# The opening of a Fourier-mixing and MLP kernel: x ahead of the weights, weights converted inside the first chunk, plain products there

## The chip, the cores and the metric

One core of one Trainium2 chip. The metric is the time of one execution on the device in microseconds (us). Spans in the traces run from the first to the last instruction and are 1.7 to 1.8 us shorter than the times. In the profile's rows PE is TensorE (PEld its weight loads), DVE is Vector, ACT is ScalarE, POOL is GpSimd and SP is SyncE; a name with q, such as ACTq, is that engine issuing transfers.

## The reference

x is (8, 3008, 256). A Fourier transform over the sequence and over the features, real part kept, gives 24,064 rows of 256. These pass an MLP with 2048 hidden units:

```python
X = np.fft.fft(np.fft.fft(x, axis=1), axis=2).real.astype(np.float32)
h = X.reshape(B * S, D) @ w_in          # weights are float64
g = h * np.clip(h + 3.0, 0.0, 6.0) / 6.0
return (g @ w_out).astype(np.float32)
```

## The kernel before

Four pairs of sequences are done in turn. For a pair: x and its mirrored rows ("partners") are read and folded; stage 1 of the sequence transform gives z, which goes to DRAM (`zd`) and comes back regrouped as g; stage 2 gives q. The transform over features is folded into the first weights (W1, and a column WN). Then come 12 chunks of 8 steps. A step is the first layer (`mlp1`: four matmuls of 256 columns, then Vector and ACT for the activation) and the second layer (`mlp2`): a 2 x 2 block product by seven products instead of eight, with additions on GpSimd (`combine`) and mixed weight blocks.

The weights arrive as float64, in 16 pieces. ACT reads out the exponent bits (`exponent_a`), PE and ACT make them a float32 power of two (`exponent_b`, `exponent_c`), Vector assembles the mantissa and multiplies (`mantissa`, `join`). Before, almost all of this ran in the opening, with x interleaved; only the end of piece 15 and the last mixing fell into the first chunk:

```python
for c in range(NXC):                       # eight chunks of x
    if c + 2 < NXC: load_x(first, c + 2)
    load_w(c + 2)                          # a weight piece beside each chunk
    fold_first(first, c) ...               # Vector
    on_scalar(c); on_vector(c)             # exponent, mantissa of piece c
    for i in range(XC // 2): stage1_first(first, c, i)
    on_tensor(c)
load_g(first, 0)
for j in range(NXC, 15):                   # the other pieces
    ...                                    # (cut)
for i in range(2): stage2(first, 0, i)
...                                        # the chunks, 8 steps each
def exponent_b(j):
    ex = ps_h.tile([P, WB], F32, tag="uv", name="ex")
    for i in range(2):
        nc.tensor.matmul(ex[:], E[:, i], PM[:, j % 2, i].bitcast(F16), ...)
```

Of the kernel before, what the change touches and what calls it, by code (L numbers as in the profile page):

```python
# [51 lines left out]

PROD = ("P1", "P2", "-P4", "P5", "P7", "-P6", "P3")
# [3 lines left out]
def kernel(  # L57
# [51 lines left out]
    F = consts.tile([PR + 2, 5 * PZ + NP * NXC + 1], F32, name="F")  # L109
# [17 lines left out]
    def x_tile(pr, i):  # L127
        pool, tag = xpool, "x"
        if pr.p == 0 and 4 <= i < 13:
            pool, tag = ((apool, "a"), (cpool, "c"), (spool, "t"))[(i >= 8) + (i >= 11)]  # L130
        return pool.tile([PR + 2, XC, D], F32, tag=tag, name="xt")
# [8 lines left out]
    def load_forward(pr, c):  # L140
        xt = x_tile(pr, 2 * c)

        nr = PR + 2 if pr.p < NP - 1 else PR
        rows = x_pn[pr.p * PR:pr.p * PR + nr]
        n = XC if c < NXC - 1 else XC - 1
        nc.gpsimd.dma_start(out=xt[0:nr, 0:n, :], in_=rows[:, c * XC + 1:c * XC + 1 + n, :])
        if n < XC:
            nc.gpsimd.dma_start(out=xt[0:nr, n:XC, :], in_=rows[:, 0:1, :])
        pr.x[c] = xt

    def load_partners(pr, c):
        xr = x_tile(pr, 2 * c + 1)
# [31 lines left out]
    def fold_first(pr, c):  # L184
        xt, xr = pr.x[c][0:PR], pr.xr[c][0:PR]
        r = xr[:, ::-1, :]
        y = ypool.tile([PR, XC + 1, D], F32, tag="y", name="y")
        tt = nc.vector.tensor_tensor
        tt(y[:, 0:XC, 1:P], xt[:, :, D - 1:P:-1], r[:, :, 1:P], op=AL.add)
        tt(xt[:, :, 1:P], xt[:, :, 1:P], r[:, :, D - 1:P:-1], op=AL.add)  # L190
        tt(xt[:, :, 0:P + 1:P], xt[:, :, 0:P + 1:P], r[:, :, 0:P + 1:P], op=AL.add)
        pr.y[c] = y

    def stage1_first(pr, c, i):
        sl = slice(2 * i, 2 * i + 2)
        a, b = pr.x[c][0:PR, sl, :], pr.y[c][:, sl, 1:P]
        ps = bank([P, 2, D], "ps1")
        for k, (f, m, c0) in enumerate([(F[0:PR, 0:PZ], a[:, :, 0:P + 1], 0), (F[0:PR, 0:PZ], b, 1),
                                        (F[0:PR, 0:PZ], a[:, :, 1:P], P + 1), (FN[0:PR], b, P + 1)]):
            nc.tensor.matmul(ps[0:PZ, :, c0:c0 + m.shape[2]], f, m, start=(k == 0), stop=(k > 0),  # L200
                             skip_group_check=True)
        evict_z(pr, c, i, ps)
        if i == XC // 2 - 1:
            del pr.x[c], pr.xr[c]
# [9 lines left out]
    def stage1(pr, c, i):  # L214

        y = pr.y[c]
        ps = bank([P, 2, D], "ps1")
# [10 lines left out]
        evict_z(pr, c, i, ps)  # L228

    def evict_z(pr, c, i, ps):  # L230
        if i == 0:

            pool, tag = (gpool, "g") if pr.p == 0 and c % 3 == 2 else (zpool, "z")
            pr.z[c] = pool.tile([PZ, XC, D], F32, tag=tag, name="z")
            if c == 0:
                pr.zd = dpool.tile([2, NK1, 2, NS, D], F32, tag="zd", name="zd")
                pr.zq = dpool.tile([2, NK1, 2, NS], F32, tag="zq", name="zq")
        z = pr.z[c]
        nc.scalar.copy(z[:, 2 * i:2 * i + 2, :], ps[0:PZ])  # L239
        if i == XC // 2 - 1:  # L240
            nc.sync.dma_start(
                out=pr.zd[:].rearrange("b k c n d -> (b k c) n d")[:, c * XC:(c + 1) * XC, :],
                in_=z[:],
            )
            turn_column(pr, c, z)
            del pr.y[c], pr.z[c]
# [4 lines left out]
    def turn_column(pr, c, z):  # L251
        n = XC if c < NXC - 1 else XC - 1
        zc = zpool.tile([PZ, XC], F32, tag="zc", bufs=4, name="zc")
        nc.scalar.activation(zc[:, 0:n], z[:, 0:n, P], AF.Identity, scale=F[0:PZ, 5 * PZ + NP * NXC:])
        cs = slice(c * XC, c * XC + n)
        nc.sync.dma_start(out=pr.zq[:, :, ::-1, cs].rearrange("b k c n -> (b k) c n"), in_=zc[:, 0:n])
        if n < XC:
            nc.sync.dma_start(out=pr.zq[:, :, :, c * XC + n].rearrange("b k c -> (b k c)"), in_=z[:, n, P])


    def load_g(pr, gr):
        g = gpool.tile([P, 2 * KK, D + 1], F32, tag="g", name="g")
        ks = slice(gr * 2 * KK, (gr + 1) * 2 * KK)
        gb = [g[b * N2:(b + 1) * N2] for b in range(2)]
        for b in range(2):
            nc.sync.dma_start(out=gb[b][:, :, 0:D], in_=pr.zd[b].rearrange("k c n d -> (c n) k d")[:, ks, :])
        for b in range(2):
            nc.sync.dma_start(out=gb[b][:, :, D], in_=pr.zq[b].rearrange("k c n -> (c n) k")[:, ks])
# [36 lines left out]
    class Chunk:  # L305
# [3 lines left out]
        def __init__(self, pr, ck):  # L309
            self.pr, self.ck = pr, ck  # L310
            self.last = ck == NCK - 1
            self.final = self.last and pr.p == NP - 1
# [81 lines left out]

    def mlp2(ch, fc):
# [78 lines left out]
    FN = wpool.tile([PR + 2, PZ], F32, tag="FN", name="FN")  # L474
# [8 lines left out]
    raw, exs, fracs, w = {}, {}, {}, {}  # L483

    def load_w(j):
        kind, n, i = PIECES[j]
        st = wpool.tile([P, 2 * WB], I32, tag="st", bufs=4, name="st")
# [17 lines left out]
    def exponent_a(j):  # L505
        top = raw[j][:].bitcast(I16).rearrange("p (n four) -> p n four", four=4)[:, :, 3]
        for i in range(2):
            low = PM[:, j % 2, i].bitcast(U8).rearrange("p (n two) -> p n two", two=2)[:, :, 0]
            nc.scalar.activation(low, top, AF.Identity, bias=bias[:, i:i + 1], scale=(1 - 2 * i) / 16.0)  # L509

    def exponent_b(j):
        ex = ps_h.tile([P, WB], F32, tag="uv", name="ex")
        for i in range(2):
            nc.tensor.matmul(ex[:], E[:, i], PM[:, j % 2, i].bitcast(F16), start=(i == 0), stop=(i == 1))  # L514
        exs[j] = ex
# [4 lines left out]
    def mantissa(j):  # L520
# [3 lines left out]
        top = wpool.tile([P, WB], I32, tag="top", bufs=2, name="top")  # L524
# [5 lines left out]
    def join(j):  # L530
# [8 lines left out]
        b12 = wpool.tile([P, 2, P], F32, tag="b12", bufs=2, name="b12")[:] if i == 0 else None  # L539
        for h, g in enumerate((block(n, 0), b12) if i == 0 else (block(n, 1), block(n, 6))):  # L540
            f, e = (t.rearrange("p (c q h e) -> h p c q e", c=2, h=2, e=DH)[h] for t in (frac, ex))
            nc.vector.tensor_tensor(g.rearrange("p c (q e) -> p c q e", e=DH), f, e, op=AL.mult)
        if i == 0:
            w[PIECES[j]] = b12
# [4 lines left out]
    def use_pair(j):  # L549
        kind, n, _ = PIECES[2 * j]  # L550
        if kind == "in":
            fold_w_in(n)
        else:
            mix_w_out(n)

    def mix_w_out(j):

        b12 = w.pop(("out", j, 0))
        g = [block(j, i) for i in range(7)]
        tt = nc.vector.tensor_tensor  # L560
        tt(g[3], g[0], b12, op=AL.subtract)
        tt(g[5], g[6], g[3], op=AL.add)
        tt(g[2], g[5], g[1], op=AL.subtract)
        tt(g[4], g[6], b12, op=AL.subtract)

    def fold_w_in(n):

        cs = slice(n * WB, (n + 1) * WB)
        ws = [w.pop(("in", n, i)) for i in range(2)]
        sums = []  # L570
        for blk in range(2):
            ps = bank([P, WB], "wps")
            for i in range(2):
                nc.tensor.matmul(ps[:], C[:, i, blk * P:(blk + 1) * P], ws[i], start=(i == 0), stop=(i == 1))  # L574
            sums.append(ps)

        def copy():
            for blk in range(2):
                nc.scalar.copy(W1[:, blk, cs], sums[blk][:])
            nc.sync.dma_start(out=wn[n:n + 1], in_=W1[P - 1:P, 1, cs])  # L580

        copies.append(copy)


    def load_wn(n):
        nb = WB // P
        nc.sync.dma_start(out=WN[:, n * nb:(n + 1) * nb], in_=wn[n].rearrange("(j p) -> p j", p=P))
# [6 lines left out]
    def keep_awake(n):  # L594
        ps = ps_h.tile([P, 2 * TB], F32, tag="uv", name="awake")
        for i in range(n):
            nc.tensor.matmul(ps[:], ones[:], Z[:], start=True, stop=True)  # L597
# [4 lines left out]
    keep_awake(6)  # L602
    nc.sync.dma_start(out=F[:], in_=c_stage1)
# [4 lines left out]
    PM = wpool.tile([P, 2, 2, WB], I16, tag="PM", name="PM")  # L608
    nc.vector.memset(PM[:].rearrange("p j i n -> p (j i n)").bitcast(I32), 0x64006400)
    nc.vector.tensor_copy(IX[:], F[:, 5 * PZ:5 * PZ + NP * NXC])  # L610
    nc.scalar.mul(FN[:], F[:, 0:PZ], -1.0)
# [3 lines left out]
    nc.sync.dma_start(out=C[:], in_=dim[:, :, 0:D])  # L615
    E = wpool.tile([P, 2, P], F16, tag="E", name="E")
    nc.scalar.copy(E[:], CE[:])
    for b in range(2):
# [3 lines left out]
    wn = dpool.tile([NWI, WB], F32, tag="wn", bufs=1, name="wn")  # L622


    load_forward(first, 0)
    load_partners(first, 0)
    load_w(0)
    load_x(first, 1)
    load_w(1)
# [3 lines left out]
    pending, copies = [], []  # L633

    def on_scalar(j):
        for i in pending:
            exponent_c(i)
        if j is not None:
            exponent_a(j)
        while copies:  # L640
            copies.pop(0)()

    def on_vector(j):
        if j is not None:
            mantissa(j)
        for i in pending:
            join(i)

    def on_tensor(j):
        if j is not None:  # L650
            exponent_b(j)
        done = pending.pop() if pending else 0
        if done % 2:
            use_pair(done // 2)
        if j is not None:
            pending.append(j)

    for c in range(NXC):
        if c + 2 < NXC:
            load_x(first, c + 2)  # L660
        load_w(c + 2)
        if c < NXC - 1:
            fold_first(first, c)
        else:
            for part in range(2):
# [185 lines left out]
```

## Time and profile before

| Kernel before | |
|---|---|
| time, median of 4 runs (first chip) | 1980.1 us |
| last operation of x's last fold starts | 49.4 us |
| first step: second half of its fused addition with WN | 82.4 us |
| E: eight steps of the first chunk done, with the first layer of two more | 132.2 us |
| from E to the end of the span (1978.3) | 1846.1 us |

Vector's timeline has the first step (columns: start, length, engine, line, operation, output <- inputs, shapes, count):

```profile
82.03 0.86 DVE L339 SCALAR_TENSOR_TENSOR s<-qn,WN,u 128x256 f32<-128x256 f32 x2
```

The two instructions of 0.47 us are merged into one row, so the second starts near 82.4. PE's timeline has E, where the last row below starts:

```profile
129.18 1.46 PE L403 MATMUL acc<-a,G 128*128 128x256 f32 x6
130.48 1.89 PE L403 MATMUL acc<-c,G 128*128 128x256 f32 x8
132.21 1.02 PE L227 MATMUL ps<-y,F 94*96 94x512 f32 x2
```

### The profile page before, as it was taken

The numbers are of one execution on the slowest core, as the hardware profiler recorded it, in microseconds if no ns is written. First come the engines' busy times: TensorE is split into PE (matmuls) and PEld (weight loads), VectorE is DVE, ScalarE is ACT, GpSimd is POOL, SyncE is SP. The second block draws the span as 40 slices with busy tenths as digits, with TensorE's granted clock in tenths as the row PEclk, the third lists the DMA queues.
The fourth block names the chain that finished last, engine by engine and source line by source line (L and its number), as shares of the span: only waits on it lengthen the run. The fifth ranks groups of instructions, "written<-read, shape, count | busy, mean of one in ns | idle before, by whom it ended". The sixth has DMA issues, their size and how long they took to land.

```text
span 1978.3 us, 27746 instructions
## 1 busy us (share of the span) xinstructions
PE 1949.1 (99%) x9178; PEld 1685.4 (85%) x9178; DVE 1433.5 (72%) x2775; ACT 687.9 (35%) x1164; POOL 1414.2 (71%) x1604
## 2 busy tenths in 40 slices
PE   8899999999999999999999999999999999999998
PEld 5588888888998888888898888888889888888887
DVE  5677767776787776776777776777678777777776
ACT  6533333333333333333333333333333333333332
POOL 4277778786687787777768877778667667666765
PEclk9999999999999999999999999999999999999999
DMA  9502211111111111221111221212110101111000
GB/s 307 136 26 61 51 41 46 49 49 35 27 36 51 41 49 48 54 59 24 36 32 30 63 55 44 56 41 54 37 22 23 30 14 25 26 24 28 17 20 20
DMA packets 149701, 93.31 MB, mean 47 GB/s; under 512 B 121739, under 2 KB 135055, under 8 KB 149558
## 3 DMA queue, kind: packets, MB, share of 16 engines
q1 hardware_dynamic: 139294, 57.86, 12.2%
q0 software_dynamic: 9472, 33.49, 5.9%
q8 instruction: 72, 1.18, 0.2%
q14 instruction: 71, 0.58, 0.1%
q10 hardware_dynamic: 792, 0.20, 0.0%
HBM read 54.19 MB, written 37.33 MB: 46 GB/s over the span
## 4 chain that ended last, share of the span: by engine, by line
PE 93%; DVE 2%; ACT 1%; issue 0%; DMA 0%; SPq 0%; DVEq 0%; ACTq 0%
PE acc L403 56%; PE v L334 16%; PE u L334 16%; PE ps L284 2%; PE ps L227 2%; DVE a L379 1%; DVE s L339 1%; ACT t L376 0%; ACT PM L509 0%; DVE o L461 0%; PE wps L574 0%; DVE u L360 0%; PE ps L224 0%; PE ex L514 0%; PE awake L597 0%
## 5 line engine op out<-in xcount | busy, mean ns | idle before, releaser
L393 POOL TENSOR_TENSOR c<-a 128x512 f32<-128x512 f32 (+1 forms) x383 | 478.2, 1248 | 431.4 <-PE acc L403 369.3
L403 PE MATMUL acc<-c,G 128*128 128x256 f32 (+1 forms) x3072 | 712.0, 375 | 0.0
L376 ACT ACTIVATE t<-u,half 128x512 f32<-128x512 f32 (+1 forms) x384 | 261.0, 680 | 1100.5 <-DVE u L349 1018.7
L403 PEld LDWEIGHTS acc<-c,G 128*128 128x128 f32 x3072 | 577.5, 190 | 72.7
L339 DVE SCALAR_TENSOR_TENSOR s<-qn,WN,u 128x256 f32<-128x256 f32 (+1 forms) x768 | 330.0, 471 | 354.3 <-PE u L334 354.0
L403 PE MATMUL acc<-a,G 128*128 128x256 f32 (+1 forms) x2304 | 551.2, 375 | 0.0
L403 PEld LDWEIGHTS acc<-a,G 128*128 128x128 f32 x2304 | 433.8, 190 | 55.9
L334 PE MATMUL v<-q,W 127*128 127x256 f32 (+1 forms) x1536 | 390.1, 376 | 4.4 <-DVE a L379 4.4
L334 PE MATMUL u<-q,W 128*128 128x256 f32 (+1 forms) x1536 | 388.3, 375 | 2.4 <-DVE a L379 2.1
L379 DVE SCALAR_TENSOR_TENSOR a<-t,u 128x512 f32<-128x512 f32 (+2 forms) x448 | 263.7, 600 | 104.9 <-ACT t L376 102.1
L334 PEld LDWEIGHTS u<-q,W 128*128 128x128 f32 x1536 | 285.7, 190 | 58.2 <-issue 14.8
L334 PEld LDWEIGHTS v<-q,W 127*128 127x128 f32 x1536 | 288.7, 190 | 45.1 <-DVE a L379 4.1
L393 POOL TENSOR_TENSOR c<-c,a 128x256 f32<-128x256 f32 (+1 forms) x383 | 274.8, 717 | 30.0
L393 POOL TENSOR_TENSOR c<-a,c 128x256 f32<-128x256 f32 (+1 forms) x383 | 274.6, 717 | 30.1
L349 DVE TENSOR_TENSOR u<-s,v 128x512 f32<-128x512 f32 x352 | 245.0, 696 | 37.7 <-PE v L334 0.8
L379 DVE SCALAR_TENSOR_TENSOR a<-t,v 128x512 f32<-128x512 f32 (+1 forms) x480 | 263.2, 564 | 0.0
L376 ACT ACTIVATE t<-v,half 128x512 f32<-128x512 f32 (+1 forms) x384 | 260.5, 678 | 0.0
L351 DVE TENSOR_TENSOR v<-v,s 128x512 f32<-128x512 f32 x352 | 243.7, 692 | 0.0
L393 POOL TENSOR_TENSOR r<-w,e 128x256 f32<-128x256 f32 (+1 forms) x94 | 90.8, 987 | 3.7
L411 ACT ACTIVATE e<-acc 128x512 f32<-128x512 f32 (+2 forms) x190 | 86.3, 545 | 3.4 <-PE acc L403 3.3
L461 DVE STREAM_TRANSPOSE o<-r 128x256 f32<-128x256 f32 (+1 forms) x192 | 72.5, 414 | 0.2
L239 ACT COPY z<-ps 96x512 f32<-96x512 f32 x64 | 37.2, 582 | 83.7 <-PE ps L227 65.2
(91 smaller groups left out, 780.2 us busy)
## 6 DMA issues: line engine op xcount, KB each, us to landing
out_dram<-o SPq DMA_DIRECT2D x746, 32.0 KB
zd<-z SPq DMA_DIRECT2D x32, 384.0 KB
g<-zd SPq DMA_DIRECT2D x48, 256.0 KB
xt<-in_x_dram POOLq DMA_DIRECT2D x21, 384.0 KB, 4.1
qn<-qd SPq DMA_DIRECT2D x19, 256.0 KB
st<-in_moe_w_in_dram POOLq DMA_DIRECT2D x8, 512.0 KB, 9.1
st<-in_moe_w_out_dram POOLq DMA_DIRECT2D x8, 512.0 KB, 5.1
xt<-in_x_dram POOLq DMA_DIRECT2D x7, 376.0 KB, 3.9
```

The source lines that it names most:

```text
L227: nc.tensor.matmul(ps[0:PZ], F[0:PR, 0:PZ], y[:, 2 * i:2 * i + 2, :], start=True, stop=True)
L284: nc.tensor.matmul(ps[:, blk, u * P:n].rearrange("p (b k) -> p b k", b=2), g[:, kk, blk * (P + 1):blk * (P + 1) + P], T[:, :, gr, blk, kk, ...
L334: nc.tensor.matmul(ps[:, i, 0:nq], W1[r, blk, f * P:(f + 1) * P], q[r, blk, of:of + nq], start=True, stop=True)
L339: nc.vector.scalar_tensor_tensor(s[:, i, 0:nq], qn[:, of:of + nq], WN[:, f:f + 1], u[:, i, 0:nq], op0=AL.mult, op1=AL.add)
L349: nc.vector.tensor_tensor(u[:], s[:], v[:], op=AL.add)
L351: nc.vector.tensor_tensor(v[:], v[:], s[:], op=AL.subtract)
L376: nc.scalar.activation(t, h, AF.Relu, bias=half[:], scale=scale)
L379: nc.vector.scalar_tensor_tensor(dst, t, 1.0, h, op0=AL.min, op1=AL.mult)
L393: (eng or nc.gpsimd).tensor_tensor(out, in0, in1, op=AL.add)
L403: nc.tensor.matmul(ch.acc[i // 2][:, i % 2, 0:ch.n], G[:, i, fc, :], mv, start=(fc == 0 and i % 2 == 0), stop=(fc == NF - 1), skip_group_c ...
L411: nc.scalar.mul(ch.e[:, k:i + 1, 0:ch.n], ch.acc[i // 2][:, 0:i + 1 - k, 0:ch.n], 1.0 / WS)
L461: nc.vector.transpose(o[:, 0:n // DH, h], ch.r[:, m, h, 0:n].rearrange("p (j i) -> p j i", i=DH))
```

## The change

The intent is to reach the first step earlier. x is read ahead of all weights; only the first four pieces are converted before the first step, and the other twelve inside the first chunk. Weights 4 and later are read only when the first group's g is back. Of z only the rows of the first group are written at once; the rest waits (`later`). Exponents of odd pieces from the fifth on are made by a subtraction on Vector instead of two matmuls. In the first chunk the second layer is done by eight plain products (four matmuls of 512 columns), since the mixed weight blocks aren't ready; mixing moves from Vector to GpSimd. WN is filled straight from W1's last row by small transfers, not over DRAM.

```diff
+    for c in ORDER[0:3]: load_x(first, c)
+    for k, c in enumerate(ORDER):
+        for part in range(2): fold(first, c, part, nc.vector)
+        for i in range(XC // 2): stage1(first, c, i)
+        keep_awake(1)
+        if k + 3 < NXC: load_x(first, ORDER[k + 3])
+        ...                                   # weights 0 to 3 behind the last x
     load_g(first, 0)
+    nc.gpsimd.tensor_copy(seen[:], first.g[0][:, 0, 0:1])   # GpSimd waits for g
+    for j in range(4, 8): load_w(j)
+    ...                                       # pieces 0 to 3 converted
     for i in range(2): stage2(first, 0, i)
+    for dst, src in later[2:6] + later[0:2] + later[6:]:
+        nc.scalar.dma_start(out=dst, in_=src)               # deferred z
     spread(first, 0)
+    fold_w_in(*folds.pop(1)); copy_all()      # W1's second half, its WN column
     def exponent_b(j):
+        if j >= 4 and j % 2:
+            nc.vector.tensor_tensor(exs[j][:], pm[0], pm[1], op=AL.subtract)
+            return
+    def mlp2_first(ch, fc):
+        for h in range(2):
+            for f in range(2):
+                nc.tensor.matmul(ch.acc[h][:], G[:, (B11, B12, B21, B22)[2 * f + h], fc, :], a[:, :, f], ...)
     # in the copy() of fold_w_in:
+            nc.sync.dma_start(out=WN[:, f:f + 1], in_=W1[P - 1:P, 1, f * P:(f + 1) * P])
     # further down:
+    DUE = [(6, 7), (8, 9, 10), (11, 12), (13, 14), (15,), (), (), ()]   # pieces per step
+            t = 2 * late + (9 - late // 4) * c   # next pair's x, in the first pair later and closer
     # (many lines cut)
```

## The prediction

> **What bounds the kernel now.** I read the page first: busy shares, then the 40 slices, then the chain that ended last.
>
> ```profile
> PE 1949.1 (99%) x9178; PEld 1685.4 (85%) x9178; DVE 1433.5 (72%) x2775; ACT 687.9 (35%) x1164; POOL 1414.2 (71%) x1604
> ...
> PE   8899999999999999999999999999999999999998
> ...
> PE 93%; DVE 2%; ACT 1%; issue 0%; DMA 0%; SPq 0%; DVEq 0%; ACTq 0%
> ```
>
> PE is 93% of the chain and the first slices alone are thin. Next, busy time by stretches of the span (columns: stretch, length, busy time and count of PE, PEld, DVE, ACT, POOL, then clock, DMA share, GB/s):
>
> ```profile
> 0.00:46.00 46.00, 42.98 (x154) 25.59 (x154) 23.93 (x53) 31.25 (x49) 19.80 (x32) 1.00 0.99 301
> 46.00:92.00 46.00, 35.59 (x115) 19.46 (x114) 30.28 (x65) 25.80 (x43) 9.12 (x12) 0.90 0.62 168
> 92.00:132.00 40.00, 38.54 (x185) 33.71 (x184) 30.98 (x52) 12.28 (x21) 25.77 (x28) 0.99 0.05 16
> 132.00:1978.00 1846.00, 1831.94 (x8730) 1606.62 (x8728) 1348.34 (x2607) 618.59 (x1054) 1359.51 (x1533) 1.00 0.16 39
> ```
>
> After 132 us (the end of the first chunk: its eighth group of second-layer matmuls runs 129.18 to 132.21) PE lacks only 14 of 1846 us. The change leaves that part's work as it is, so the time after is 1846 plus the moment E at which the first chunk is done. The question is how far E moves from 132.2.
>
> Three landmarks before E, from the timeline by engine: the last fold of x starts at 46.56 and ends at 49.5; Vector's first step of the first chunk starts at 82.0; E = 132.2. In the first 46 us DMA is full (share 0.99). In the second stretch it is ACT, PE and Vector in turn, seen in the chain in order of time:
>
> ```profile
> 68.81 0.47 issue
> 69.28 1.41 ACT PM L509 x2
> 70.69 0.04 issue
> 70.73 0.39 PE ex L514
> ...
> 71.64 1.41 ACT PM L509 x2
> 73.05 0.04 issue
> 73.09 0.39 PE ex L514
> ...
> 74.00 1.41 ACT PM L509 x2
> 75.41 0.04 issue
> ```
>
> ACT's two exponent instructions come every 2.36 us: that is the price of one of the 16 weight pieces while nothing useful can run on PE.
>
> **What the Trainium skill says.** "DMA: Bandwidth & Descriptors", Issuing engines are not separate DMA queues: transfers of all engines interleave on the same 16 DMA engines, whoever issued them. The trace agrees: an indirect read of x takes a median of 5.1 us to land over the whole span and 12.5 us in the first 90 us, beside the weights. So moving weights behind x buys x time. "TensorE: Matmul & The Clock Gate", Part 1: after about 3.4 us of idleness the array runs at half clock until busy again for about as long. The trace agrees: after 3.3 us idle the two-pass 512-column matmul at 49.17 took 1.99 us, against 1.02 us at 132.21. "SBUF — State Buffer", Who interferes with whom: a Vector operation with two SBUF inputs contends with GpSimd reading SBUF. Agrees: Vector's weight mixing (256 columns) took 0.42 us at 70.07 and 1.11 us at 100.84, beside GpSimd's additions. The changed kernel gives this mixing to GpSimd.
>
> **Part 1, x phase.** Before, a chunk of x (forward and partner rows, 384 KB each) is folded every 4.5 to 6 us, waiting for DMA (16.6 us in seven waits). After, weights leave the way until x is issued. First fold: the index table is now a small transfer of its own, so the first partner read still issues near 3.9 us; it landed at 9.1 before, beside weights; I take 8.3. Vector's fold grows from three operations to the five of the general form: four of 0.68 us, 0.61 from start to start, plus 0.17, 2.6 us a chunk (2.9 for the special one, now first). Buffers hold three chunks, so chunk k+3 is issued when k is folded. Three chunks cost 2.6 (fold) + 1.5 (GpSimd issues 0.55 and 0.95) + about 5 (landing) = 9.1 us, 3.0 a chunk. Eight chunks: 8.3 + 2.9 + 7 x 3.0 = 32.2, and since the first three run back to back at 2.6, about 31.5. **Gain: 49.4 - 31.5 = 18 us.** PE needs 2 x 0.86 + 0.43 (keep-awake), ACT 2 x 0.58 + 0.3 a chunk: neither binds.
>
> **Part 2, from the last fold to the first step.** Before it is 82.0 - 49.4 = 32.6 us with nine pieces of weights in it. After, only four pieces: stage 1 and its eviction until 34.4; then on ACT in order four pieces at 1.41 + 0.57 = 7.9, one copy of folded weights 0.6, two copies of q after stage 2 (1.5, with PE's 0.87 and 0.89 ahead of each): 44.4. Beside this runs the first group's round trip through DRAM: write at 34.4, about 2.3 to land, two reads at 0.62 each to issue and about 2.3 to land: 40.2, hidden by the pieces. Then ACT issues eight deferred writes of z (0.32 each if as on SP): 47.0; copies qn (47.6) and the second half of folded weights (48.2); its last row goes to WN through a small transfer of about 2.3 us. First step on Vector at **50.5**. This stretch becomes 19.0 instead of 32.6: **gain 13.6 us.**
>
> **Part 3, the first chunk.** Now it carries twelve pieces and six half-folds of weights, and plain products. Before: 132.2 - 82.0 = 50.2 us. After, by engine:
> - Vector: eight steps at 3.7 (82.03 to 85.72 in the trace) = 29.6; twelve mantissas at 1.07 = 12.8; four joins of 0.61, eight of 0.70 (two halves) = 8.0; six subtractions in place of the matmul pair, about 0.6 each = 3.6. Sum 54.0. Behind it at the end PE's 1.7 + 3.45 + 1.73. Floor 61.
> - PE: eight steps of 1.73 (first layer) + 3.45 (eight products of 256 columns, written as four of 512, where seven took 3.02) = 41.4; six exponents at 0.87 = 5.2; six half-folds at 1.73 = 10.4; two early first-layer steps and one stage-2 half 4.3. Sum 61.
> - ACT: eight times 1.3 + twelve times (1.41 + 0.57) + six copies of 0.6 = 38.
>
> Two engines both near 61, chained with ACT: they will not overlap perfectly. Laid out in the program's order I find waits: pieces 4 and 5 hold Vector about 2.3 us (ACT reaches their exponents after its other work), then PE's queue holds piece 12's exponent behind a product that needs piece 11 joined, about 4.3 us, and Vector and PE alternate. The full layout reaches 73, but it puts each operation at its whole duration and in few cases two early; I take **69**, between the floor and that. **Loss: 69 - 50.2 = 18.8 us.**
>
> One half of stage 2 moves behind E (0.9 more after). The rest cancels: a mix of the last pair of weights and some loads fall into slack.
>
> **Sum.** -18 - 13.6 + 18.8 + 0.9 = about -12 us: E near 120, the time 1979.9 - 12 = **1968 us**, 0.6% less.
>
> **Rivals.**
> - *The first chunk costs only its floor* (61): E near 111.5 and 1960 us. For: Vector and PE have nearly equal sums and a lead of two pieces. Against: before, where Vector alone was late by one join, PE waited 2.1, 1.8 and 1.5 us in steps 0 to 3.
> - *The deferred work comes back whole*: Vector becomes the bound of the first chunk with ACT's waits in it, PE's gaps drop its clock (0.85 before in 90 to 100 us), 3.45-us products run at half speed, and the chunk takes 80: E near 131, the time 1979, nothing gained. For: Vector would be near 54 of 69 us busy with waits on ACT between almost all of it. Against: the order was laid out step by step for this.
> - *The round trip binds*: g and the weights behind it come late, since weights 4 to 7 wait for g on GpSimd, with 2.6 MB of deferred z in the same DMA engines. If weight 4 lands after 53, each us of lateness delays all. At 300 GB/s four pieces are 7 us after 43, so it is probably just in time; it would make 1972.
> - *x stays latency-bound* at 3.5 us a chunk: T0 is later by 3 us, 1971.
>
> **Range and chances.** The three parts have errors of about 3, 4 and 7 us; together some 8.5. Eight in ten: 1955 to 1977. Faster by over 2% needs 39.6 us, that is E below 92.6: with the first step at 50.5 the chunk would need 42 us, under the 54 of Vector alone and the 61 of PE. Slower by 2% would need E at 172. Each gets 0.01.
>
> **What would show it right or wrong.** In the changed kernel: last fold of x ends at 30 to 34 (wrong if beyond 38: then x isn't freed by the order); first fused addition with WN on Vector at 48 to 54; eight products done, with the first layer of two more steps, at 113 to 128; Vector over 75% busy in between, with ACT's exponent as its releaser; PE's clock under 1 in places there; after E, 1846 +- 3 us to the end. If that last number moves, a part that I took as untouched has changed, and the prediction is wrong in its frame. If the chunk takes under 60 us, my count of Vector is wrong.

## The result, and the profile after

The changed kernel took 1985.0 us (median of 4 runs; 1984.6 to 1987.1) where the kernel before took 1980.1. The ratio is 1.0026, interval 1.0008 to 1.0043. By the 2% rule it is the same; the time lies outside the predicted range of 1955 to 1977 about 1968.

From the page of the changed kernel (busy shares, slices of PE, chain):

```profile
PE 1942.2 (98%) x9094; PEld 1668.9 (84%) x9094; DVE 1441.5 (73%) x2780; ACT 686.3 (35%) x1163; POOL 1398.6 (71%) x1592
...
PE   9699999999999999999999999999999999999998
...
PE 92%; DVE 4%; ACT 2%; DMA 1%; issue 1%; POOL 0%; DVEq 0%; SPq 0%; ACTq 0%; POOLq 0%
```

PE has 7 us less to do, the first slice is fuller than before and the second thinner (9 and 6, where both were 8): the hole moved. The same stretches as in the prediction (start and end, length, busy time and count of PE, PEld, DVE, ACT, POOL, then clock, DMA share, GB/s):

```profile
0.00:46.00 46.00, 41.42 (x125) 19.11 (x126) 29.90 (x64) 25.68 (x42) 17.00 (x28) 1.00 0.82 225
46.00:92.00 46.00, 32.17 (x119) 22.48 (x119) 27.78 (x50) 22.57 (x37) 10.67 (x16) 0.89 0.65 208
92.00:132.00 40.00, 35.13 (x115) 20.39 (x114) 30.29 (x57) 18.91 (x32) 7.80 (x10) 1.00 0.12 32
132.00:1983.00 1851.00, 1833.45 (x8739) 1606.88 (x8738) 1353.48 (x2612) 619.16 (x1053) 1363.14 (x1541) 1.00 0.16 39
```

PE's busy time in the second stretch fell from 35.59 to 32.17 us and in the third from 38.54 to 35.13: PE fills these stretches less, though the first step came earlier. The landmarks, from the timelines:

| | before | after | difference of the piece that ends here |
|---|---|---|---|
| last fold of x | 49.4 | 34.2 | -15.2 |
| first step | 82.4 | 60.6 | -6.6 |
| E | 132.2 | 132.5 | +22.1 |
| end of span | 1978.3 | 1983.0 | +4.4 |

E after is where the first of these two rows of PE's timeline starts; the wait of 1.54 us in the second comes back in experiment 10:

```profile
132.46 1.03 PE L336 MATMUL u<-q,W 128*128 128x256 f32 x4
135.03 1.13 PE L336 MATMUL v<-q,W 127*128 127x256 f32 x4 [1.54 <-DVE a L381]
```

So the first step did come 22 us earlier, and all of it was given back in the first chunk; 4.4 us were added behind it, in the part that I had taken as untouched.

Why the first step is at 60.6 and not earlier shows in ACT's timeline, then Vector's (the bracket is the idle time just before and what ended it; "ACTq" is the issuing of DMA from ACT's queue):

```profile
46.80 4.94 ACTq L706 DMA_DIRECT2D zd<-z  x8
51.78 0.58 ACT L298 COPY qn<-ps 128x512 f32<-128x512 f32 x1 [4.40 <-DMA zd<-z]
52.26 0.59 ACT L594 COPY W<-wps 128x512 f32<-128x512 f32 x1
```

```profile
53.65 0.48 DVE L341 SCALAR_TENSOR_TENSOR s<-qn,WN,u 128x256 f32<-128x256 f32 x1 [7.39 <-PE u L336]
60.59 0.48 DVE L341 SCALAR_TENSOR_TENSOR s<-qn,WN,u 128x256 f32<-128x256 f32 x1 [6.46 <-DMA WN<-W]
```

ACT is held 4.9 us by issuing the eight deferred writes before it can copy the weights that feed the column. The first half of the fused addition runs at 53.65. The second waits 6.46 us for the column of WN, 512 bytes, which was released by the copy's end at 52.85: 7.7 us for a transfer that I had put at 2.3. In those microseconds the DMA engines are full:

```profile
52.00:56.00 4.00, 3.09 (x14) 2.75 (x15) 0.48 (x1) 0.85 (x2) 0.00 (x0) 1.00 1.00 395
56.00:60.00 4.00, 1.93 (x9) 1.44 (x9) 0.00 (x0) 0.00 (x0) 0.00 (x0) 1.00 1.04 415
```

Inside the first chunk, from the first step to E, one stretch says what the engines did:

```profile
60.10:132.50 72.40, 58.96 (x189) 35.89 (x189) 57.84 (x105) 39.33 (x65) 16.12 (x20) 0.93 0.30 84
```

PE is busy 81% (part of it at a reduced clock, 0.93 in the mean), Vector 80%, ACT 54%. None is full. Much of the waiting of Vector and ACT is for each other, or for PE: in Vector's timeline, for instance, piece 12's join waits for an exponent that ACT could only finish when PE had got past the products of the third step:

```profile
101.20 0.75 DVE L567 TENSOR_TENSOR G<-top,ex 128x256 f32<-128x256 f32 x2 [3.65 <-ACT ex L544]
```

A rival, that the weights come too late for the chunk, the trace sets aside: past the first step no compute engine's wait in this stretch ended with the landing of a weight.

### The profile page after: what moved, and what is told of

Read it like the earlier page. It is cut to its first block, busy times and chain, and to the rows that moved or that the text cites. A ratio compares the mean times of both kernels' runs of the same rounds, so it can differ in the third digit from the quotient of the medians.

```text
span 1983.0 us, 27541 instructions
## 1 busy us (share of the span) xinstructions
PE 1942.2 (98%) x9094; PEld 1668.9 (84%) x9094; DVE 1441.5 (73%) x2780; ACT 686.3 (35%) x1163; POOL 1398.6 (71%) x1592
## 4 chain that ended last, share of the span: by engine, by line
PE 92%; DVE 4%; ACT 2%; DMA 1%; issue 1%; POOL 0%; DVEq 0%; SPq 0%; ACTq 0%; POOLq 0%
PE acc L421 55%; PE v L336 16%; PE u L336 16%; PE ps L213 2%; PE ps L285 2%; DMA xt<-in_x_dram,IX 1%; DVE a L381 1%; DVE s L341 1%; PE acc L405 1%; ACT t L378 1%; ACT PM L531 0%; DVE o L479 0%; DVE u L362 0%; DMA zd<-z 0%; PE spare L590 0%
## 5 line engine op out<-in xcount | busy, mean ns | idle before, releaser
L395 POOL TENSOR_TENSOR c<-a 128x512 f32<-128x512 f32 (+1 forms) x375 | 467.6, 1247 | 409.7 <-PE acc L421 348.6
L421 PE MATMUL acc<-c,G 128*128 128x256 f32 (+1 forms) x3008 | 697.0, 374 | 0.0
L421 PEld LDWEIGHTS acc<-c,G 128*128 128x128 f32 x3008 | 565.3, 190 | 71.2 <-POOL c L395 0.2
L421 PE MATMUL acc<-a,G 128*128 128x256 f32 (+1 forms) x2256 | 538.8, 374 | 0.0
L421 PEld LDWEIGHTS acc<-a,G 128*128 128x128 f32 x2256 | 423.3, 190 | 55.0
L395 POOL TENSOR_TENSOR c<-a,c 128x256 f32<-128x256 f32 (+1 forms) x375 | 268.3, 715 | 29.4
L395 POOL TENSOR_TENSOR c<-c,a 128x256 f32<-128x256 f32 (+1 forms) x375 | 268.1, 715 | 29.4
L213 PE MATMUL ps<-y,F 94*96 94x512 f32 x120 | 61.3, 601 | 5.2 <-ACT q L288 5.2
```

The source lines that it names most:

```text
L213: nc.tensor.matmul(ps[0:PZ], F[0:PR, 0:PZ], y[:, 2 * i:2 * i + 2, :], start=True, stop=True)
L395: (eng or nc.gpsimd).tensor_tensor(out, in0, in1, op=AL.add)
L421: nc.tensor.matmul(ch.acc[i // 2][:, i % 2, 0:ch.n], G[:, i, fc, :], mv, start=(fc == 0 and i % 2 == 0), stop=(fc == NF - 1), skip_group_c ...
```

## The experiments

Two questions: why the first step is at 60.6, and why the chunk takes 72 us. For the first, theory A says that the column waits its turn behind bulk transfers; rival B that 128 pieces of 4 bytes are slow by themselves. For the second, theory A says that the chunk is a chain over Vector, ACT and PE; rival C that PE's sum of work binds.

All rows below are read from the trace of one run each. "Column" is from the end of the copy that feeds it to the second half of the fused addition. Ratios are to the kernel before on the same chip (its medians were 1981.8, 1982.8, 1982.4 and 1979.9 in the four groups of runs). The part from E to the end was 1850.2 to 1850.7 us in every run that didn't touch it, and the chunk was 71.85 to 71.9 in the three runs that left its code alone (changed, writes behind, slots apart), so it can be read to half a us or better, finer than the timed ratio. The first step is less steady: where nothing ahead of it was changed it lay between 59.9 and 62.2, in one run at 64.6.

| run | first step | column | first step to E | E | E to end | ratio |
|---|---|---|---|---|---|---|
| before | 82.4 | | 49.8 | 132.2 | 1846.1 | 1 |
| changed | 60.6 | 7.7 | 71.9 | 132.5 | 1850.5 | 1.0026 |
| writes behind | 58.3 | 8.1 | 71.9 | 130.2 | 1850.6 | 1.0003 |
| weights behind column | 58.8 | 2.7 | 76.2 | 134.9 | 1850.7 | 1.0021 |
| column first | 52.3 | 2.0 | 73.5 | 125.8 | 1850.7 | 0.9970 |
| exponents 12 and 14 early | 62.2 | | 72.9 | 135.1 | 1850.6 | 1.0038 |
| exponent 12 only | 59.9 | | 70.5 | 130.4 | 1850.6 | 1.0003 |
| exponents all on PE | 60.0 | | 75.0 | 135.0 | 1850.4 | 1.0031 |
| half the products | 61.0 | | 64.5 | 125.4 | 1850.7 | 0.9980 |
| ACT's exponent twice | 61.8 | | 76.5 | 138.3 | 1850.5 | 1.0035 |
| no fraction | 60.2 | | 67.0 | 127.2 | 1850.2 | 0.9988 |
| slots apart | 60.2 | | 71.9 | 132.1 | 1847.0 | 0.9996 |
| seven products | 64.6 | | 94.9 | 159.5 | 1850.3 | 1.0132 |
| combined | 52.0 | 2.0 | 72.4 | 124.3 | 1846.9 | 0.9961 |

**1. Deferred writes behind the column.**

```diff
-    for dst, src in later[...]: nc.scalar.dma_start(out=dst, in_=src)
     spread(first, 0)
     fold_w_in(*folds.pop(1)); copy_all()
+    for dst, src in later[...]: nc.scalar.dma_start(out=dst, in_=src)
```

> Only the eight deferred writes of z move: behind the copy of the second half of folded weights, so behind the issue of the WN column. In the changed kernel ACT spends 4.9 us issuing them ahead of that copy, and the second WN column takes from 52.9 to 60.6 us to come. Theory A (the column waits its turn in DMA engines filled with z and weights): copy of folded weights ends near 48, the column lands in 3 to 5 us since only weights 4 to 9 are ahead of it, first step at 51 to 53, first chunk as long as before (72), whole time 7 to 9 us less than the changed kernel, 1976 to 1978. Rival B (the column is slow by itself, 128 pieces of 4 bytes, 7.7 us whatever else runs): first step at 55 to 56, 5 us less, 1980.

The copy came earlier, though it ended at 50.2 and not near 48, but the column still needed 8.1 us, and the first step was at 58.3. Taken alone this spoke for B, whose 55 to 56 it also missed. The whole time was 1982.2 us, above what either had expected. ACT's timeline shows that the issuing itself now took 9.1 us:

```profile
49.63 9.08 ACTq L709 DMA_DIRECT2D zd<-z  x8
59.70 0.69 ACT L378 ACTIVATE t<-u,half 128x512 f32<-128x512 f32 x1 [9.48 <-DMA zd<-z]
```

Weights 4 to 9 (3.1 MB) had been issued from 45 us on, and the writes ran beside the column, so there was still bulk in front.

**2. Weights behind the column.**

```diff
-    nc.gpsimd.tensor_copy(seen[:], first.g[0][:, 0, 0:1])      # before piece 0
-    for j in range(4, 8): load_w(j)
     fold_w_in(*folds.pop(1)); copy_all()
+    nc.gpsimd.tensor_copy(seen[:], WN[:, NF:NF + 1])
+    for j in range(4, 10): load_w(j)
     # (cut: 8 and 9 are no longer read by pieces 0 and 1)
```

> Only weights 4 to 9 move: they are issued when the second WN column has landed, instead of when the first group's g has landed; deferred writes of z stay. Theory A: the column has 2.6 MB of z ahead of it instead of 5.7 MB of z and weights, so lands 2 to 4 us earlier (57 to 58.5), but weight 4 is then issued at 57 to 58 and lands near 60 to 61, in time for Vector's first mantissa (3.7 us after the first step): 2 to 4 us less. Rival B (slow by itself): the column lands at 60.6 as before and weights come late, so 1 to 3 us more.

Here the eight writes took ACT 8.2 us to issue, so the copy ended at 56.1; by then most of their bytes had gone. The column landed 2.7 us later:

```profile
58.76 0.48 DVE L341 SCALAR_TENSOR_TENSOR s<-qn,WN,u 128x256 f32<-128x256 f32 x1 [0.86 <-DMA WN<-W]
```

```profile
52.00:56.00 4.00, 0.00 (x0) 0.00 (x0) 0.00 (x0) 0.96 (x2) 0.00 (x0) 0.85 0.84 255
56.00:60.00 4.00, 3.84 (x9) 3.12 (x10) 1.62 (x4) 0.11 (x1) 0.88 (x2) 0.50 0.30 83
```

The same transfer, 2.7 us at a DMA share of 0.30 against 7.7 at 1.00: rival B falls. The chunk became 4.3 us longer, so the whole gained nothing clear. Weights 4 to 9 came late: Vector and ACT wait 1.7 us each for them. Also, two half-folds (16 of PE's matmuls), which the changed kernel does from 54.3 us while it waits for the column, fall behind the first step here. The rows also show PE's clock at 0.50 after PE had been idle for 6.4 us (until 56.16), which fits the Trainium skill's "TensorE: Matmul & The Clock Gate", Part 1.

**3. Both bulk streams behind the column.** Weights 4 and 5 stay where they were; weights 6 to 9 wait for the column; SP issues the writes behind the column.

```diff
-    for j in range(4, 8): load_w(j)
+    for j in (4, 5): load_w(j)
     spread(first, 0)                       # the writes ahead of it removed
     fold_w_in(*folds.pop(1)); copy_all()
+    for dst, src in later[...]: nc.sync.dma_start(out=dst, in_=src)
+    nc.gpsimd.tensor_copy(seen[:], WN[:, NF:NF + 1])
+    for j in range(6, 10): load_w(j)
     # (cut: 8 and 9 as in run 2)
```

> The earlier run with weights behind the column had the column land 2.6 us after its issue, against 7.7 in the changed kernel and 8.6 with only the writes moved, so theory A stands and rival B is dropped. Here both bulk streams go behind the column: only weights 4 and 5 are issued with the first group's g; the deferred writes of z are issued by SP behind the column and not by ACT; weights 6 to 9 when the column has landed. Theory A: column issued near 50.3, landed 2.6 to 4 us later, first step at 53 to 54.5 against 60.6, chunk as long as before or 1 us longer (72 to 73.5), whole time 5 to 7.5 us less than the changed kernel, that is 0.999 to 1.000 of the kernel before. If the chunk eats it (weights 6 to 9 late), the first step moves but the end does not.

```profile
49.67 0.58 ACT L594 COPY W<-wps 128x512 f32<-128x512 f32 x1 [1.14 <-PE wps L590]
```

```profile
52.25 0.48 DVE L341 SCALAR_TENSOR_TENSOR s<-qn,WN,u 128x256 f32<-128x256 f32 x1 [0.72 <-DMA WN<-W]
```

The column took 2.0 us, even less than expected, and the first step came 8.3 us earlier. The chunk took 1.6 us more, with most of the two half-folds of run 2 in it, so E is 6.7 us earlier. The time is 1977.3 against 1982.4 for the kernel before on that chip, 0.9970 (0.9954 to 0.9987): clear of noise and below the kernel before, though by the 2% rule still the same. A is shown for the first step.

**4 and 5. Exponent ahead of the products.** In the third step PE's queue has piece 12's exponent behind products that wait for piece 11.

```diff
+            for j in due[1:2]: exponent_b(j)        # run 4: in every step; run 5: only piece 12
             mlp2_first(*chunk(s))
-            for j in due[1:2]: exponent_b(j)
```

> Only the PE exponent of the step's second piece moves ahead of that step's products (pieces 12 and 14). In the changed kernel PE waits 2.5 us for piece 11 inside the third step's products, then ACT waits 3.1 us for piece 12's exponent and Vector 3.65 us for ACT. Theory A (the first chunk is a chain over ACT, Vector and PE in which such a hold counts in full): the chunk shrinks by 3 to 4 us and the whole time by as much. Rival C (the chunk is bound by PE's sum of work): nothing, within 1 us.

> The run with pieces 12 and 14 early lost the gain: at piece 14 the products of the fourth step then waited 2.9 us for ACT. Here piece 12 alone goes ahead of the products. From that run's third step, where the products ended 39.1 us after the first step against 39.4, I expect only 1 to 2 us less in the chunk, not the 3 to 4 of the waits seen: the hold was in parallel with PE's other work. Rival: each us of a wait counts, 3 to 4 less.

The first came out 1.1 us longer in the chunk instead of 3 to 4 shorter. The trace shows the cause: one step later piece 14 now holds the products, since ACT has not got to it:

```profile
106.08 0.39 PE L541 MATMUL ex<-PM,E 128*128 128x512 f16 x1 [2.93 <-ACT PM L531]
```

With piece 12 alone the chunk is 1.3 us shorter, as I then expected. Two waits of 3.1 and 3.65 us that look like a gain of that size were worth 1.3. That other work of the chain ran meanwhile is the likely reason; no run shows it alone.

**6. All exponents on PE.**

```diff
-        if j >= 4 and j % 2:
+        if False:
```

> The alternation is undone: odd pieces' exponents go to PE as well, instead of a Vector subtraction of 0.6 us. Theory A (chain over ACT and Vector): Vector loses 6 x 0.6 = 3.6 us, but each odd exponent now waits behind PE's products in its queue, as piece 12 does: between 3 us less and 8 us more, I expect 3 more. Rival C (PE bound): 6 x 0.87 = 5 us more.

3.1 us more in the chunk. The alternation on PE and Vector is worth that much and should stay.

**7, 8, 9. Which engine binds the chunk?** Work is taken from or given to one engine at a time: half of the products left out (wrong result), ACT's second exponent instruction done twice, Vector's second mantissa operation left out (wrong result), the last two for pieces 4 to 15.

```diff
-            for f in range(2):                                   # run 7, in mlp2_first
+            for f in range(1):
-        for i in range(2):                                       # run 8, in exponent_a
+        for i in (0, 1) if j < 4 else (0, 1, 1):
-        nc.vector.scalar_tensor_tensor(frac, lo, ...)            # run 9, in mantissa
+        if j < 4:
+            nc.vector.scalar_tensor_tensor(frac, lo, ...)
```

> Wrong result on purpose: of the first chunk's four 512-column products a step only two run, so PE has 8 x 1.73 = 13.8 us less to do; Vector and ACT do what they did. Theory A (the first chunk is bound by the chain of Vector and ACT): the end of the chunk moves by less than a third, 0 to 4 us. Rival C (PE's sum binds): 10 to 14 us less.

> Right result; for pieces 4 to 15 ACT does the second exponent instruction twice, 12 x 0.66 = 7.9 us more on ACT. Theory A (the chain runs through ACT's exponents between Vector's steps): 4 to 8 us more. If ACT has slack (39 of 72 us busy) and only Vector binds: 0 to 2 us more.

> Wrong result on purpose: pieces 4 to 15 leave out Vector's second mantissa operation, 12 x 0.61 = 7.3 us less on Vector, which is 58 of 72 us busy in the first chunk. Theory A with Vector as the main link of the chain: 5 to 7 us less. If ACT or PE bind: 0 to 2 us.

| engine | work changed, as counted beforehand | by busy time in the chunk | chunk changed | share of the first (of the second) |
|---|---|---|---|---|
| PE | -13.8 us | -10.9 | -7.4 | 0.54 (0.68) |
| ACT | +7.9 | +8.9 | +4.6 | 0.59 (0.52) |
| Vector | -7.3 | -8.4 | -4.85 | 0.66 (0.58) |

The counted work is the number of operations by their time from start to start. PE's busy time fell less than that as its clock fell too: 0.89 in the mean of run 7's chunk against 0.93, and 670 ns for a product against 594. In run 8 the clock was 0.89 as well, and PE was busy 2.7 us longer with the same work.

Neither C nor my form of A holds: PE's share is above the third that A allowed and below what C asked, and Vector's 4.85 is just under the 5 to 7 expected. By either count all three engines have a share of more than half: each us of the work touched counts for 0.5 to 0.7 us at E. That rules out that one engine alone binds the whole chunk, and fits a chain that passes through all three in turn. It is not proof of such a chain: the clock moved with the work, and the shares hold for the operations touched only (for all busy time of the three they would add up to over 90 us, in a chunk of 72).

**10. Next pair's first stage off the steps of stage 2.** Both use the one PSUM bank for such work. In the first pair the change puts stage 1 at steps 16, 24, ... and 19, 27, ..., while stage 2 comes at 19, 23, 35, 39, ....

```diff
-                t = 2 * late + (9 - late // 4) * c
+                t = 2 * late + late // 4 + (9 - late // 4) * c
```

> The next pair's first stage is moved by one step in the first pair, so that it doesn't fall on steps that have stage 2, which share one PSUM bank. In the changed kernel PE waits 5.2 us in 8 waits for the copy of q there (3.7 in 6 before). Expected: 4 or fewer waits, 2.6 us or less, time 1 to 2 us less; too small for the timed ratio, to be read in the waits. The first chunk is not touched.

PE's waits from E on, changed kernel, then this run (sum in us, times, longest):

```profile
PE ps L213 <- ACT q L288: 5.2, 8, 0.7
PE v L336 <- DVE a L381: 2.7, 5, 1.5
```

```profile
PE v L336 <- DVE a L381: 2.7, 5, 1.5
PE ps L213 <- ACT q L288: 2.5, 4, 0.7
```

The stretch from E to the end fell from 1850.5 to 1847.0 us, where 1 to 2 less were expected. These waits account for 2.7 of the 3.5; the other 0.8 is in PE's busy time (1832.99 to 1832.18 with the same count of 8737), for which I have no cause.

1847.0 is the 1846.1 of before plus the 0.9 us of the half of stage 2 that moved behind E, but that is a coincidence. The kernel before has such waits too:

```profile
PE ps L227 <- ACT q L287: 3.7, 6, 0.7
PE v L334 <- DVE a L379: 1.1, 4, 0.5
```

So of the 4.4 us that the changed kernel has more than the kernel before, 1.5 are waits that the new step numbers add, 1.6 are waits for Vector, and 1.3 are PE's busy time, 0.9 of it the moved half. Nearly all of the 1.6 is the one wait of 1.54 us right behind E that is shown above: it lies at the hand-over from the first chunk, where PE has caught up with Vector, and experiment 10 leaves it in place. What experiment 10 gains, it gains by placing the stage better than the kernel before did.

**11. Seven products in the first chunk.** The plain products are undone; for this the half-folds had to share the bank of stage 1, as the two spare ones are needed, and moved to the steps 1 and 2.

```diff
-            mlp2_first(*chunk(s))
+            if s in (0, 2, 4, 6): mix_w_out(s // 2)
+            combine(*chunk(s)); mlp2(*chunk(s))
-        ps = ... spare[len(copies) % 2]
+        ps = bank([P, 2, nb], "wps")
     # (more lines cut)
```

> The part of the change with eight plain products is undone: the first chunk is done by seven products as the others are, with GpSimd mixing the weights and combining the activations ahead of each step's products; folds of the weights take the one PSUM bank of stage 1 instead of two spare ones. PE has 3.45 us less. Theory A: the chain gets GpSimd's combination (2.7 us) and mixing (2.9 us in every second step) as new links, 1 to 6 us more. Rival C (PE's sum binds): 3.5 us less.

23 us more in the chunk, where A had 1 to 6 more and C 3.5 less. PE's timeline shows the main wait, 9 us in the first step, until GpSimd had issued weight loads, which waited for Vector and ACT, and then mixed:

```profile
89.57 1.22 PE L421 MATMUL acc<-a,G 128*128 128x256 f32 x2 [9.07 <-POOL G L579]
```

It is not a clean measure: the shared bank adds 11.6 us of PE waits for ACT's copies of the folded weights. It shows that this form is worse, not what the plain products alone are worth.

**12. Combined.** Runs 3, 5 and 10 together, and the fold that feeds the column ahead of PE's `spread`.

```diff
-    spread(first, 0)
     fold_w_in(*folds.pop(1)); copy_all()
+    spread(first, 0)
     # and the edits of runs 3, 5 (piece 12 only) and 10
```

> The three edits that helped or cost nothing, together: both bulk streams behind the WN column, piece 12's exponent ahead of the third step's products, the next pair's first stage off stage 2's steps; also the fold that feeds the column goes ahead of PE's spread, so that the copy is 0.9 us earlier and the column with it. Expected by adding: first step at 51.5 (52.25 less 0.9 for the fold, if qn's copy, now behind, doesn't take it back), chunk 71 to 73 us instead of 73.5 (piece 12's hold cost 5.3 us of waiting there), 1 to 2 us less after it (waits for the copy of q 2.5 instead of 5.2 us). Whole time 1972 to 1976 on the chip where the kernel before takes 1980, a ratio of 0.996 to 0.998. Rival: the three overlap and nothing beyond the column's 0.997 appears.

```profile
51.96 0.48 DVE L341 SCALAR_TENSOR_TENSOR s<-qn,WN,u 128x256 f32<-128x256 f32 x1 [0.27 <-DMA WN<-W]
```

1971.1 us against 1979.9, 0.9961 (0.9947 to 0.9975), the best: 0.4% faster than the kernel before. The earlier fold gave 0.3 us instead of 0.9 (qn's copy at 50.28 is now level with the column); chunk and remainder came as the runs add up.

## Why the prediction was wrong

It said 12 us less; it was 4.7 us more in the spans. By its own steps:

- **Part 1, x phase.** A gain of 18: measured 15.2. The mechanism held (DMA gave way, Vector waited for x 8.4 us instead of 16.6), and the first fold started at 8.3 as worked out. The term too small was the landing time: 6.6 us in the median for a partner read, where I took 5. So a chunk of x took 3.3 us and not 3.0, near the rival "x stays latency-bound".
- **Part 2, to the first step.** "gain 13.6 us": measured 6.6. This is the step that failed most, by 7 us, through two terms. "eight deferred writes of z (0.32 each if as on SP)", 2.6 us, took ACT 4.9. "a small transfer of about 2.3 us" took 7.7. The rival with 2.6 MB of z in the DMA engines named the right traffic and the wrong victim: I asked if weight 4 would come late, and not what the same bytes do to the column that the first step waits for. Runs 1 to 3 show it: 7.7 and 8.1 us behind bulk, 2.7 and 2.0 without.
- **Part 3, the first chunk.** "69", taken between the floor of 61 and the full layout of 73: measured 71.9. The full layout was nearer, and the allowance taken off it for pessimism was the larger error. With the first step near 52 (runs 3 and 12), as the prediction had it, the chunk took 73.5 and 72.4. The floor of 61 by either engine is not reached as work on any of three engines counts at E (runs 7 to 9). Vector 80% busy and PE's clock under 1 came as said.
- **"after E, 1846 +- 3 us to the end"**: measured 1850.5. The frame, a remainder untouched, failed by 3.5 us beyond the 0.9 that I had moved there: 1.5 from the new step numbers of the next pair, which I did not read, 1.6 from waits for Vector, nearly all of it one wait at the hand-over from the first chunk, and 0.4 in PE's busy time (experiment 10).
- **The sum.** In lengths, 2.7 + 7.4 (26.4 instead of 19.0 us) + 2.9 + 3.5 = 16.5 us, against 12 + 4.7 = 16.7 missed; the rest is rounding. Every error is on the same side. The range was made as if the parts' errors were independent; most were the omission of waits. The rival "The deferred work comes back whole" had E near 131 and nothing gained, close to what came, but by another way: a first step at 50.5 and a chunk of 80, where 60.6 and 71.9 were measured. Its number is luck.
- The chance of 0.01 for faster by over 2%, and the argument for it, held: no run's first chunk took less than the 54 us counted for Vector alone.
- Three readings of the kernel before were off, with no weight in the sum: PE was idle 2.87 us before the matmul at 49.17, not 3.3 (the clock was 0.50 from there on, so the half clock came after less idleness than the 3.4 us cited); chunks of x were folded every 4.4 to 6.7 us, not 4.5 to 6; and 82.0 is the first half of the first step, where the part before it ends at 82.4 by the landmark used here.

## What to carry to other kernels

Moving work out of an opening pays only what the place that takes it has spare: here the 22 us gained came back inside the first chunk, where three engines share the work on each piece and each counts. When bulk transfers are deferred, ask which small transfer on the critical path is issued behind them; letting one 512-byte column go first was worth 6.7 us at E. And a wait in a trace is not what its removal gains: waits of 3 to 4 us in the chunk were worth 1.3, while 2.7 us of waits fewer behind E came with a gain of 3.5.

## What the Trainium skill lacked or had wrong

- "DMA: Bandwidth & Descriptors", Queues, rings and completion order, says that an engine takes its queue rows in turn, packet by packet. From that one would expect a small transfer on SP's own row to pass bulk on other rows soon. The runs: 7.7 and 8.1 us with megabytes on the rows of ACT and GpSimd, 2.0 and 2.7 us with little. How long a small DMA takes beside bulk on other rows is not given there.
- The same page, Issuing engines are not separate DMA queues, calls the time to initiate a transfer usually small relative to the transfer. Here eight writes of 321 KB, one behind the other, held ACT for 4.9, 8.2 and 9.1 us, 0.6 to 1.1 us each, and SP for 7.0 in run 3. Full DMA engines alone are not the cause: in the kernel before SP issued single writes of 384 KB between 14.9 and 42.3 us in 0.30 to 0.34 us each, at a DMA share of 0.99. That it comes of issuing eight in a row is a guess that no run here tests.
- Checked and found right: "VectorE: DVE Perf Modes", What auto-detection actually checks, asks that every tensor be 16-bit for the doubled two-source rate; the subtraction of two 16-bit tensors into float32 took 0.69 us for 512 columns, the same as float32 operands.
